# The end of a fused attention and convolution kernel reordered: quotients given out once their accumulators are complete, the last PV product ahead, output rows summed in banks of their own

## The chip, the cores and the metric

The kernel runs on one core of a Trainium2 chip. The metric is device time in microseconds, the median of three runs; lower is better. The program is one launch, about 51,000 instructions, written in a language in which each engine gets its instructions in the order in which the Python code issues them, and waits on semaphores for what other engines produce.

## The reference, cut to what matters

Two independent parts share the output: attention goes to columns 0 to 511, a long convolution to columns 512 to 1023.

```python
# A: 32 query heads of width 16 share one key and one value head; S = 2048, D = 512
q = (x @ wq).reshape(B, S, 32, 16).transpose(0, 2, 1, 3)
k, v = x @ wk, x @ wv
p = softmax(einsum("bhqd,bkd->bhqk", q, k) * 16 ** -0.5)
a = einsum("bhqk,bkd->bhqd", p, v).transpose(0, 2, 1, 3).reshape(B, S, 512) @ wo
# B: kv = (4-tap causal convolution of k) * v;  y = 2048-tap causal convolution of kv (by FFT) + kv * D
b = q_in * y
out = concatenate([a, b], axis=-1)
```

## The kernel before

**Stacks and tiles.** Attention is cut into 32 stacks: four chunks of 512 query rows, and in each chunk eight groups of four heads. A stack has 32 tiles (a few have 30). For one tile TensorE computes scores of 128 keys against two heads and 512 queries (`scores`, L934), ScalarE takes the exponential of the whole 128 x 1024 block (`exp`, L946), and TensorE multiplies by the values (`pv`, L970). The value matrix carries a column of ones, so the same product gives the softmax denominators. The last stack (number 31) is cut the other way: tiles 0 to 15 do all four heads for its first 256 queries, tiles 16 to 31 for its last 256. At the end of a stack, or of a half of the last one, VectorE adds the two accumulators into `ao` (L979, L980).

**Quotients.** For the stacks up to 29 numerators and denominators go through DRAM (`heads`). For the last two stacks `over` (L1190) does it on VectorE alone: six instructions on 128 x 256 (transpose, maximum, reciprocal, copy, transpose, product). Stack 30 (`ao2`) takes two calls, one for each half of its columns; stack 31 takes one for each half as it ends. The two halves of tile `lr` hold the quotients of stack 30 and of the first half of stack 31, tile `lb` those of its second half.

**Output rows.** The output projection (`wo`) adds up in `wp`, four tiles of 128 rows x 512 for the last chunk: heads of stacks 24 to 27 first, then of 28 and 29 (`wo_rows(i, [14])`, product `f<-wo,o`, VectorE L1171), then of stack 30 (product `f<-wl,lr`, VectorE L1184). `last` does the share of stack 31 after everything else: products of `lr` or `lb` with `wl` (L231), sums to `y`, four DMAs of 256 KB.

**Order.** `attend` (L1037) walks over the tiles. For tile x it issues the scores and the exponential of tile x+2, the planned `pv`, and then `fill.turn`, which lets a list of generator threads issue their own TensorE and VectorE work, as far as a slot's room goes. The first thread in the list that is willing goes first: `own` is first, `wo_part` sixth. A `yield` with a count asks for TensorE room, `yield 0, n` for VectorE time. Before, `own` ended after stack 30's special tile, and `wo_part` issued the calls of `over` for stack 30 and for the first half of stack 31 where they came in its own sequence.

**PSUM.** `wide` gives a two-bank tile of a pool with two buffers (tag `s`, shared with the scores), `pair` one of another pool with two buffers (tag `f`). In the last stack one `pair` is the accumulator of `pv` and the other goes from one filling product to the next, so a product that opens such a tile waits until VectorE has read the one before. The sums of `last` took three `wide` tiles in turn and one `pair`, each of which held one output row tile.

Of the kernel before, what the change touches and what calls it, by code (L numbers as in the profile page):

```python
# [8 lines left out]
F32 = mybir.dt.float32  # L9
# [5 lines left out]
ALU = mybir.AluOpType  # L15
# [4 lines left out]
P = 128  # L20
S = 2048
D = 512
H = 32
DH = 16
NKT = S // P
NQ = 4 * H // 4
CB = 256
# [78 lines left out]
WAIT = -1.0  # L106
# [3 lines left out]
class _Emit:  # L110
# [892 lines left out]
    def own(self):  # L1003

        nc, v = self.nc, self.nc.vector
        c = [x / TWO[5] * (-(2.0**18)) ** (5 - i) for i, x in enumerate(TWO)]
        self.vo = self.msk[:, 163:195]
        done = [f"q{c}" for c in range(4)]
        yield from self.after(*done)
        yield 0, 100  # L1010
        v.tensor_scalar(self.vo, self.vx[:, OWN, :], -TWO[5] * 2.0 ** (DOWN - 90), None, ALU.mult)
        room = [self.w.tile([P, 2, 4, 512], F16, tag="xt", bufs=2, name=self.nm("own")) for _ in range(2)]
        self.po = room[0].rearrange("p i k n -> p (i k n)").bitcast(F32).rearrange("p (a e n) -> p a e n", a=2, e=2)
        f = room[1].rearrange("p i k n -> p (i k n)").bitcast(F32).rearrange("p (a e n) -> p a e n", a=2, e=2)
        for n in OWN_IN:
            while self.slot < 32 * n - 32 + OWN_AT or self.owed:
                yield WAIT, 1
            for a in range(2):
                yield (1, 2400, CONT, 1, 4) if a else (1, 2400, NEW, 1)
                b = self.pair()  # L1020
                self.keys(b, n, OWN, a, slice(0, 512))
                v.tensor_scalar(self.po[:, a], b, MAGIC, None, ALU.add)
                v.scalar_tensor_tensor(f[:, a], self.po[:, a], MAGIC, b, ALU.subtract, ALU.subtract)
                if a == 0:
                    yield WAIT, 1.5, CONT
            for a in range(2):
                g, y = self.po[:, a], f[:, a]
                x = self.w.tile([P, 2, 512], I16, tag="s2", bufs=S2, name=self.nm("x"))
                yield 0, 900
                v.tensor_scalar(x, g, 2.0**-11, (127 - DOWN) * 128 - MAGIC * 2.0**-11, ALU.mult, ALU.add)  # L1030
                for i in range(4, -1, -1):
                    yield 0, 1220
                    v.scalar_tensor_tensor(g, g if i < 4 else y, c[i], y if i else x.bitcast(BF16), ALU.add, ALU.mult)  # L1033
            self.owed = [(-1 - n, part) for part in range(2)]
        self.seen.add("own")

    def attend(self, fill):  # L1037
        self.od = self.dr.tile([NQ, P, 512], F32, name="od")
# [82 lines left out]
    def wo_part(self):  # L1121
        nc, w, I = self.nc, self.w, self.I
        xr = self.out.rearrange("b (c p i) d -> (b c) p i d", c=4, p=P, i=4)
        for c in range(2):
            yield from self.after(("oc", 4 * c + 3), *[("cx", 1)] * c)
            for i in (0, 2):
                b = yield from self.wo_rows(i, range(4 * c, 4 * c + 4), 1400)
                for r in range(2):
                    t = self.s2("wp", (512,))
# [7 lines left out]
        for i in (0, 2):  # L1137
            b = yield from self.wo_rows(i, range(8, 11), 1400)
# [4 lines left out]
        for i in (0, 2):  # L1143
            b = yield from self.wo_rows(i, [11], 1400)
            for r in range(2):
                t = self.s2("wp", (512,))
# [7 lines left out]
        for i in (0, 2):  # L1154
            b = yield from self.wo_rows(i, range(12, 14), 1400)
# [4 lines left out]
        for q in range(2):  # L1160
            t = self.s2("wl", (512,))
            nc.gpsimd.memset(t, 0.0)
            for j in range(4):
                h = H - 8 + 4 * q + j
# [3 lines left out]
        for i in (0, 2):  # L1168
            b = yield from self.wo_rows(i, [14], 1400)
            for r in range(2):  # L1170
                nc.vector.scalar_tensor_tensor(self.wp[i + r], b[r], 1 / (OS * WS), self.wp[i + r], ALU.mult, ALU.add)  # L1171
        both = w.tile([P, 2, 4, 512], F32, tag="in", bufs=1, name="lr")
        t, self.lr = both[:, 0], both[:, 1]
        for h in range(2):
            while self.slot < 2 * NKT * (NQ - 1) + 1:
                yield WAIT, 1
            yield 0, 1800
            self.over(self.ao2[:, 256 * h : 256 * h + 256], t, h)
        halves = [slice(256 * h, 256 * h + 256) for h in range(2)]
        for i in (0, 2):  # L1180
            work = [[(h, t[:, 2, r * P : (r + 1) * P], self.wl[0][:, h]) for h in halves] for r in (i, i + 1)]
            b = yield from self.halves(*work, 2, 1400)
            for r in range(2):
                nc.vector.tensor_tensor(self.wp[i + r], self.wp[i + r], b[r], ALU.add)  # L1184
        while self.slot < 2 * NKT * (NQ - 1) + NKT:
            yield WAIT, 1
        yield 0, 1800
        self.over(self.ao[:, 0:256], self.lr, 0)

    def over(self, a, t, h):  # L1190

# [11 lines left out]
    def last(self, fill):  # L1203

        nc = self.nc
        xr = self.out.rearrange("b (c p i) d -> (b c) p i d", c=4, p=P, i=4)
        fill.finish()
        t = self.w.tile([P, 2, 4, 512], F32, tag="big", bufs=2, name="lb")[:, 0]
        self.pv(len(self.at) - 2, None)
        s = [self.wide()[:, 0, :]]  # L1210
        y = [self.s2("y", (512,)) for _ in range(4)]
        rows = lambda x, i: x[:, 2, i % 2 * P : (i % 2 + 1) * P]
        self.mm(s[0], rows(self.lr, 0), self.wl[1])
        self.pv(len(self.at) - 1, None, True)
        self.over(self.ao[:, 256:512], t, 0)
        s += [self.wide()[:, 0, :], self.wide()[:, 0, :], self.bank()]
        self.mm(s[1], rows(self.lr, 1), self.wl[1])
        self.mm(s[2], self.ident, self.wp[2], stop=False)
        for i in range(2, 4):
            self.mm(s[i], rows(t, i), self.wl[1], start=i > 2)  # L1220
        for i in range(2):
            nc.vector.tensor_tensor(y[i], self.wp[i], s[i], ALU.add)
        nc.scalar.copy(y[2], s[2])
        nc.vector.tensor_tensor(y[3], self.wp[3], s[3], ALU.add)
        for i in range(4):
            (nc.sync, nc.scalar)[i // 2 % 2].dma_start(xr[3][:, i, 0:D], y[i])


class _Fill:
# [226 lines left out]
```

## Time and profile before

| | us |
|---|---|
| median of three runs | 1016.74 (1013.69, 1016.74, 1018.21) |
| profiled execution, its own time | 1014.1 |
| its span, first to last instruction | 1012.3 |
| TensorE busy, share of the span | 947.4, 94% |
| ScalarE busy | 953.3, 94% |
| VectorE busy | 738.7, 73% |
| GpSimd busy | 172.0, 17% |
| mean granted TensorE clock | 0.989 |

In the rows of the timeline the columns are start, length (from the first start to the last end of the merged instructions), engine, line, operation, output and inputs, shape, count, and in brackets the idle time before it on that engine with what the profile takes for its releaser. "issue" is a wait that the profile ties to no other engine. One 512-column float32 product of L231 is four instructions in the order, one for each 32 output rows, and eight records in the trace. A table of windows gives busy time by engine in each stretch, then the granted TensorE clock as a share of full speed.

### The profile page before, as it was taken

How to read it: one execution, taken by the hardware profiler on the slowest of the kernel's cores; microseconds unless marked ns; L12 is line 12 of the kernel's file. 1: busy time of each engine (PE TensorE's matmuls, PEld its weight loads, DVE VectorE, ACT ScalarE, POOL GpSimd, SP SyncE). 2: the span in 40 equal slices, each digit the busy share in tenths (PEclk: the TensorE clock that was granted, in tenths of full speed). 3: DMA queues.
4: the chain of work that ended last, by engine and by line, in shares of the span. 5: the costliest groups of instructions: out<-in, count | busy, mean ns of one | idle time of the engine just before them, and what ended most of it. 6: DMA issues, size and time to landing. Idle time of an engine off the chain costs nothing.

```text
span 1012.3 us, 51279 instructions
## 1 busy us (share of the span) xinstructions
PE 947.4 (94%) x23439; PEld 463.1 (46%) x23439; DVE 738.7 (73%) x1009; ACT 953.3 (94%) x1034; POOL 172.0 (17%) x305
## 2 busy tenths in 40 slices
PE   8999999999999999999999989999889989998985
PEld 4344455444454444445554545544334445443452
DVE  4647866998538888989988858598999942866633
ACT  4699999999999999999999989999999999999982
POOL 2443111411003000101233434000000023200000
PEclk9899999999999999999999999999999999999998
DMA  7262333432123211122154424101211143310101
GB/s 231 92 190 75 119 103 102 107 99 84 46 75 78 70 53 54 53 90 75 55 152 123 126 86 124 54 22 47 70 37 43 42 126 115 92 56 25 42 4 46
DMA packets 69317, 83.12 MB, mean 82 GB/s; under 512 B 20800, under 2 KB 58278, under 8 KB 69094
## 3 DMA queue, kind: packets, MB, share of 16 engines
q1 hardware_dynamic: 47142, 43.51, 13.6%
q0 software_dynamic: 20320, 35.46, 11.8%
q8 instruction: 185, 3.03, 1.3%
q10 hardware_dynamic: 1632, 0.81, 0.3%
q14 instruction: 38, 0.31, 0.1%
HBM read 54.66 MB, written 25.03 MB: 79 GB/s over the span
## 4 chain that ended last, share of the span: by engine, by line
PE 56%; ACT 27%; DVE 9%; issue 7%; DMA 2%; POOL 0%; SPq 0%; ACTq 0%; DVEq 0%; POOLq 0%
ACT p L946 26%; PE f L970 26%; PE s L934 16%; PE f L249 12%; DVE own L1033 2%; DVE sp L169 1%; DMA xb<-in_A_x 1%; DVE ao L979 1%; PE x L231 0%; PE f L617 0%; DVE u L218 0%; DVE sp L289 0%; DVE sp L219 0%; DVE sp L220 0%; DVE ao L980 0%
## 5 line engine op out<-in xcount | busy, mean ns | idle before, releaser
L946 ACT ACTIVATE p<-s 128x1024 f32<-128x1024 f32 x1018 | 940.8, 1068 | 22.2 <-PE s L934 19.3
L970 PE MATMUL f<-p,vx 64*32 64x512 f32 (+1 forms) x8896 | 554.0, 556 | 1.7 <-DVE cut L683 1.1
L934 PE MATMUL s<-st,kst 49*32 49x512 f16 x8144 | 431.0, 382 | 31.2 <-ACT p L946 27.6
L934 PEld LDWEIGHTS <-kst 49*32 49x32 f16 x8192 | 199.0, 89 | 396.5 <-issue 355.4
L970 PEld LDWEIGHTS f<-p,vx 64*32 64x32 f32 x8896 | 178.3, 106 | 30.0 <-issue 4.3
L169 DVE TENSOR_TENSOR sp<-sp 128x1024 f32<-128x1024 f32 x96 | 111.3, 1214 | 0.0
L289 DVE COPY sp<-f 128x512 f32<-128x512 f32 x64 | 41.2, 685 | 63.8 <-PE f L249 63.8
L294 POOL DMA_DIRECT2D ff<-in_ff x64 | 34.5, 544 | 284.4 <-ACT p L946 282.1
L249 PE MATMUL f<-wo,o 64*32 64x512 f16 x1440 | 57.4, 375 | 3.8 <-DVE r L467 1.6
L979 DVE COPY ao<-f 128x512 f32<-128x512 f32 (+1 forms) x33 | 22.2, 673 | 50.3 <-PE f L970 50.3
L169 DVE TENSOR_TENSOR sp<-sp,sp 128x1024 f32<-128x1024 f32 x48 | 55.9, 1213 | 0.2
L249 PE MATMUL f<-xT,wq 64*32 64x512 f16 x1344 | 51.8, 375 | 1.6 <-DVE gm L729 1.3
L294 POOL DMA_DIRECT2D fi<-in_fi x32 | 17.6, 555 | 187.1 <-ACT p L946 187.1
L249 PE MATMUL f<-a,ff 64*32 64x256 f32 x1024 | 43.4, 382 | 4.6 <-DMA ff<-in_ff 3.4
L467 DVE TENSOR_TENSOR r<-f,q 128x256 f32<-128x256 f32 x32 | 12.1, 419 | 45.2 <-PE f L249 45.2
L249 PE MATMUL f<-hT,ff 64*32 64x256 f32 x1024 | 41.5, 377 | 1.2 <-PE s L934 0.3
L249 PE MATMUL f<-sp,fi 64*32 64x256 f32 x1024 | 40.4, 376 | 0.4 <-PE s L934 0.4
L469 POOL DMA_DIRECT2D out<-r x32 | 17.5, 552 | 106.2 <-DVE r L467 105.9
L404 DVE TENSOR_TENSOR a<-a,t 128x512 f32<-128x512 f32 x48 | 33.2, 691 | 1.6
L395 DVE TENSOR_TENSOR t<-kk,tpb 128x512 f32<-128x512 f32 (+1 forms) x50 | 32.9, 662 | 0.7 <-DMA qd<-qp 0.7
L249 PEld LDWEIGHTS <-o 64*32 64x32 f16 x1440 | 22.5, 93 | 19.0 <-DVE r L467 2.1
L322 POOL DMA_DIRECT2D hin<-in_B_ssm_k x32 | 21.1, 665 | 58.8 <-ACT p L946 57.4
(165 smaller groups left out, 726.5 us busy)
## 6 DMA issues: line engine op xcount, KB each, us to landing
ff<-in_ff POOLq DMA_DIRECT2D x64, 128.0 KB, 2.7
od<-ao SPq DMA_DIRECT2D x60, 128.0 KB
qd<-qp SPq DMA_DIRECT2D x48, 128.0 KB
st<-qd SPq DMA_DIRECT2D x62, 98.0 KB
kk<-in_B_k POOLq DMA_DIRECT2D x32, 128.0 KB, 3.0
v<-in_B_v POOLq DMA_DIRECT2D x32, 128.0 KB, 3.2
hin<-in_B_ssm_k POOLq DMA_DIRECT2D x32, 128.0 KB, 5.5
fi<-in_fi POOLq DMA_DIRECT2D x32, 128.0 KB, 3.4
```

Source lines behind the costliest of these rows:

```text
L169: v.tensor_tensor(part(out), part(a), part(b), op)
L249: y = self.nc.tensor.matmul(out[j : j + 32, cols], w[r, j : j + 32], x[r], start=half == m == 0, stop=half == 1 and m == k - 1,)
L289: self.nc.vector.tensor_copy(c[:, :, m + i, :], b[i].rearrange("p (q n) -> p q n", q=2))
L294: self.paced(self.nc.gpsimd.dma_start(t[:, i], self.I[n][:, 2 * m2 + i]))
L322: self.paced(nc.gpsimd.dma_start(dst, src))
L395: nc.vector.tensor_tensor(out[:, n], kk[:, x], tap(i, n.stop - n.start), ALU.mult)
L404: nc.vector.tensor_tensor(a, a, t, ALU.add)
L934: self.nc.tensor.matmul(s[j : j + 32, e, :], self.kst[rows, k * P + j : k * P + j + 32], self.st[n][rows, a, cols], start=True, stop=True,)
L946: self.exps[u % 4] = self.nc.scalar.activation(self.pt[u], s, AF.Exp, scale=LN2 * DH**-0.5 / SC / SC)
L970: nc.tensor.matmul(self.acc[e][32 * j : 32 * j + 32, m], vx[rows, :], y, start=k == 0, stop=stop)
L979: nc.vector.tensor_copy(a, self.acc[0][:, m])
L1033: v.scalar_tensor_tensor(g, g if i < 4 else y, c[i], y if i else x.bitcast(BF16), ALU.add, ALU.mult)
```

## The change

Three things move. The calls of `over` for stack 30 and for the first half of stack 31 are now issued by thread `own`, the first in the list, as soon as the walk has passed the tile that completes the accumulator; `wo_part` waits for the flag `"lt"` only. In `last`, the products for output rows 0 and 1 go to the two banks of one `pair`; the first of them stands ahead of the last two `pv`, and row 0 gets its `wp` by a product with the identity in place of a VectorE sum, as row 2 had already. The last `pv`, the sums into `ao` and `over` for `lb` follow, and on TensorE the products that don't need `lb` stand behind the last `pv` and ahead of those that do. Row 3 is done in two halves of 256 columns, each in a bank of its own `wide` tile with a DMA of its own; row 0 is copied out by ScalarE.

```diff
@@ own
         self.seen.add("own")
+        yield from self.after(("cx", 1))
+        both = self.w.tile([P, 2, 4, 512], F32, tag="in", bufs=1, name="lr")
+        self.lt, self.lr = both[:, 0], both[:, 1]
+        while self.slot < 2 * NKT * (NQ - 1) + 1:
+            yield WAIT, 0.5
+        for h in range(2):
+            yield 0, 1800
+            self.over(self.ao2[:, 256 * h : 256 * h + 256], self.lt, h)
+        self.seen.add("lt")
+        while self.slot < 2 * NKT * (NQ - 1) + NKT:
+            yield WAIT, 0.5
+        yield 0, 1800
+        self.over(self.ao[:, 0:256], self.lr, 0)
@@ wo_part
-        both = w.tile([P, 2, 4, 512], F32, tag="in", bufs=1, name="lr")
-        t, self.lr = both[:, 0], both[:, 1]
-        for h in range(2):
-            while self.slot < 2 * NKT * (NQ - 1) + 1:
-                yield WAIT, 1
-            yield 0, 1800
-            self.over(self.ao2[:, 256 * h : 256 * h + 256], t, h)
+        yield from self.after("lt")
...
-        while self.slot < 2 * NKT * (NQ - 1) + NKT:
-            yield WAIT, 1
-        yield 0, 1800
-        self.over(self.ao[:, 0:256], self.lr, 0)
@@ last
-        self.pv(len(self.at) - 2, None)
-        s = [self.wide()[:, 0, :]]
...
-        self.mm(s[0], rows(self.lr, 0), self.wl[1])
+        b = self.pair()
+        s = [b[:, 0, :], b[:, 1, :]]
+        self.mm(s[0], rows(self.lr, 0), self.wl[1], stop=False)
+        self.pv(len(self.at) - 2, None)
         self.pv(len(self.at) - 1, None, True)
         self.over(self.ao[:, 256:512], t, 0)
-        s += [self.wide()[:, 0, :], self.wide()[:, 0, :], self.bank()]
+        self.mm(s[0], self.ident, self.wp[0], start=False)
         self.mm(s[1], rows(self.lr, 1), self.wl[1])
+        s += [self.wide()[:, 0, :], self.wide()]
         self.mm(s[2], self.ident, self.wp[2], stop=False)
-        for i in range(2, 4):
-            self.mm(s[i], rows(t, i), self.wl[1], start=i > 2)
-        for i in range(2):
-            nc.vector.tensor_tensor(y[i], self.wp[i], s[i], ALU.add)
+        self.mm(s[2], rows(t, 2), self.wl[1], start=False)
+        nc.scalar.copy(y[0], s[0])
+        nc.sync.dma_start(xr[3][:, 0, 0:D], y[0])
+        nc.vector.tensor_tensor(y[1], self.wp[1], s[1], ALU.add)
+        nc.sync.dma_start(xr[3][:, 1, 0:D], y[1])
         nc.scalar.copy(y[2], s[2])
-        nc.vector.tensor_tensor(y[3], self.wp[3], s[3], ALU.add)
-        for i in range(4):
-            (nc.sync, nc.scalar)[i // 2 % 2].dma_start(xr[3][:, i, 0:D], y[i])
+        nc.scalar.dma_start(xr[3][:, 2, 0:D], y[2])
+        for i, h in enumerate((slice(0, CB), slice(CB, D))):
+            self.mm(s[3][:, i, 0:CB], rows(t, 3), self.wl[1][:, h])
+            nc.vector.tensor_tensor(y[3][:, h], self.wp[3][:, h], s[3][:, i, 0:CB], ALU.add)
+            nc.sync.dma_start(xr[3][:, 3, h], y[3][:, h])
```

Up to the last stack every engine has the same instructions in the same order with the same waits. Where they differ, the order of instructions shows it. VectorE before, from the sum of stack 30's accumulators (`ao`) to the first quotient of that stack (`lr`); `f_22028` and `f_22217` are the products of stacks 28 and 29 for output rows 0 and 1, and 2 and 3:

```order
L980 TENSOR_TENSOR ao_22064<-ao_22064,f_21475 128x512
L1171 SCALAR_TENSOR_TENSOR wp_20714<-f_22028,wp_20714 128x512
L1171 SCALAR_TENSOR_TENSOR wp_20715<-f_22028,wp_20715 128x512
L1171 SCALAR_TENSOR_TENSOR wp_20716<-f_22217,wp_20716 128x512
L1171 SCALAR_TENSOR_TENSOR wp_20717<-f_22217,wp_20717 128x512
L1195 STREAM_TRANSPOSE lr<-ao_22064 128x256
L1197 TENSOR_SCALAR lr<-lr 128x8
L1198 RECIPROCAL lr<-lr 128x8
L1199 COPY lr<-lr 128x256
L1200 STREAM_TRANSPOSE lr<-lr 128x256
L1201 TENSOR_TENSOR lr<-ao_22064,lr 128x256
```

The same place on VectorE now (`f_22029` is what was `f_22028`):

```order
L980 TENSOR_TENSOR ao_22065<-ao_22065,f_21475 128x512
L1198 STREAM_TRANSPOSE lr<-ao_22065 128x256
L1200 TENSOR_SCALAR lr<-lr 128x8
L1201 RECIPROCAL lr<-lr 128x8
L1202 COPY lr<-lr 128x256
L1203 STREAM_TRANSPOSE lr<-lr 128x256
L1204 TENSOR_TENSOR lr<-ao_22065,lr 128x256
L1184 SCALAR_TENSOR_TENSOR wp_20714<-f_22029,wp_20714 128x512
L1184 SCALAR_TENSOR_TENSOR wp_20715<-f_22029,wp_20715 128x512
```

The first quotient stands ahead of the sums for rows 0 and 1; the second, of the other 256 columns, stands behind them and ahead of the sums for rows 2 and 3. In the same way the quotient of stack 31's first half now stands ahead of the four sums that add stack 30 to `wp`, where it stood behind them.

TensorE at the end before, from the third-last `pv` on; `p_22810` is the last exponential's output, `x` tiles come from `wide`, `f` tiles from `pair`:

```order
L970 MATMUL f_22544<-p_22756,vx 32x256 x8
L970 MATMUL f_22544<-p_22775,vx 32x256 x8
L231 MATMUL x_22829<-wl_21929,lr 32x512 x4
L970 MATMUL f_22544<-p_22810,vx 32x256 x8
L231 MATMUL x_22854<-wl_21929,lr 32x512 x4
L231 MATMUL x_22855<-wp_20716,ident 32x512 x4
L231 MATMUL x_22855<-wl_21929,lb 32x512 x4
L231 MATMUL f_22856<-wl_21929,lb 32x512 x4
```

And now (`f_22825` is the new pair for rows 0 and 1, which takes the buffer of the last filling product; `x_22863` is row 3's tile):

```order
L970 MATMUL f_22550<-p_22762,vx 32x256 x8
L231 MATMUL f_22825<-wl_21930,lr 32x512 x4
L970 MATMUL f_22550<-p_22781,vx 32x256 x8
L970 MATMUL f_22550<-p_22810,vx 32x256 x8
L231 MATMUL f_22825<-wp_20714,ident 32x512 x4
L231 MATMUL f_22825<-wl_21930,lr 32x512 x4
L231 MATMUL x_22862<-wp_20716,ident 32x512 x4
L231 MATMUL x_22862<-wl_21930,lb 32x512 x4
L231 MATMUL x_22863<-wl_21930,lb 32x256 x8
```

One 512-column product with the identity is added. The row-0 product stands ahead of two `pv` in place of one, and three products that don't need `lb` stand together behind the last `pv`. Of the eight instructions of the last row the first four are row 3's first half and the others its second; by its semaphores the second half waits for the VectorE sum that reads the first half out of the same tile. The first row's product waits for the last VectorE sum that reads the filling product before it.

More of the change, by code (lines that the diff above doesn't have):

```diff
@@ L1171, in wo_part @@
                 nc.vector.scalar_tensor_tensor(self.wp[i + r], b[r], 1 / (OS * WS), self.wp[i + r], ALU.mult, ALU.add)
-        both = w.tile([P, 2, 4, 512], F32, tag="in", bufs=1, name="lr")
-        t, self.lr = both[:, 0], both[:, 1]
-        for h in range(2):
-            while self.slot < 2 * NKT * (NQ - 1) + 1:
-                yield WAIT, 1
-            yield 0, 1800
-            self.over(self.ao2[:, 256 * h : 256 * h + 256], t, h)
+        yield from self.after("lt")
         halves = [slice(256 * h, 256 * h + 256) for h in range(2)]
         for i in (0, 2):
-            work = [[(h, t[:, 2, r * P : (r + 1) * P], self.wl[0][:, h]) for h in halves] for r in (i, i + 1)]
+            work = [[(h, self.lt[:, 2, r * P : (r + 1) * P], self.wl[0][:, h]) for h in halves] for r in (i, i + 1)]
             b = yield from self.halves(*work, 2, 1400)
```

## The prediction

> **What bounds the kernel now.** The page first: ScalarE's exponentials, one per tile, fill the span.
>
> ```profile
> span 1012.3 us, 51279 instructions
> L946 ACT ACTIVATE p<-s 128x1024 f32<-128x1024 f32 x1018 | 940.8, 1068 | 22.2 <-PE s L934 19.3
> ```
>
> They take 940.8 of 1012.3 us, with 22.2 us of idle time ahead of them. Up to the last stack no instruction changes its place, so only that stack and what follows the last exponential can move. There I read ScalarE's timeline from 970 us on:
>
> ```profile
> 970.81 1.97 ACT L946 ACTIVATE p<-s 128x1024 f32<-128x1024 f32 x2
> 975.22 1.94 ACT L946 ACTIVATE p<-s 128x1024 f32<-128x1024 f32 x2 [2.44 <-PE s L934]
> 978.22 15.09 ACT L946 ACTIVATE p<-s 128x1024 f32<-128x1024 f32 x16 [1.05 <-PE s L934]
> 1005.42 0.59 ACT L1223 COPY y<-x 128x512 f32<-128x512 f32 x1 [12.11 <-PE x L231]
> ```
>
> Three facts: a hole of 2.44 us, a second of 1.05, and a last exponential that ends at 978.22 + 15.09 = 993.31. From there to the end, 1012.3 - 993.31 = 19.0 us, no exponential is left. The holes wait for scores, so TensorE's timeline comes next, and with it VectorE's.
>
> ```profile
> 965.66 0.41 PE L934 MATMUL s<-st,kst 49*32 49x512 f16 x8
> 966.32 0.41 PE L249 MATMUL f<-wo,o 64*32 64x512 f16 x8
> 966.53 0.41 PE L934 MATMUL s<-st,kst 49*32 49x512 f16 x8
> 971.22 0.63 PE L970 MATMUL f<-p,vx 64*32 64x256 f32 x16
> 974.05 0.64 PE L249 MATMUL f<-wl,lr 64*32 64x256 f32 x10 [2.21 <-issue]
> 991.91 1.20 PE L970 MATMUL f<-p,vx 64*32 64x256 f32 x32
> 995.57 1.65 PE L231 MATMUL x<-wl,lr 128*32 128x512 f32 x8 [2.46 <-issue]
> 997.15 1.11 PE L970 MATMUL f<-p,vx 64*32 64x256 f32 x16
> 998.19 1.60 PE L231 MATMUL x<-wl,lr 128*32 128x512 f32 x8
> 1002.18 1.45 PE L231 MATMUL x<-wp,ident 128*32 128x512 f32 x8 [2.39 <-DVE y L1222]
> 1003.33 2.01 PE L231 MATMUL x<-wl,lb 128*32 128x512 f32 x8
> 1005.03 1.63 PE L231 MATMUL f<-wl,lb 128*32 128x512 f32 x8
> ```
>
> ```profile
> 962.18 0.69 DVE L980 TENSOR_TENSOR ao<-ao,f 128x512 f32<-128x512 f32 x1
> 970.48 1.29 DVE L1171 SCALAR_TENSOR_TENSOR wp<-f,wp 128x512 f32<-128x512 f32 x2 [6.38 <-PE f L249]
> 971.69 0.43 DVE L1195 STREAM_TRANSPOSE lr<-ao 128x256 f32<-128x256 f32 x1
> 973.42 0.42 DVE L1201 TENSOR_TENSOR lr<-ao,lr 128x256 f32<-128x256 f32 x1
> 975.49 0.43 DVE L1201 TENSOR_TENSOR lr<-ao,lr 128x256 f32<-128x256 f32 x1
> 980.14 0.42 DVE L980 TENSOR_TENSOR ao<-ao,f 128x256 f32<-128x256 f32 x1
> 992.00 1.28 DVE L1184 TENSOR_TENSOR wp<-wp,f 128x512 f32<-128x512 f32 x2 [9.96 <-PE f L249]
> 994.94 0.42 DVE L1201 TENSOR_TENSOR lr<-ao,lr 128x256 f32<-128x256 f32 x1
> 998.37 0.42 DVE L979 COPY ao<-f 128x256 f32<-128x256 f32 x1 [3.00 <-PE f L970]
> 1001.02 0.42 DVE L1201 TENSOR_TENSOR lb<-ao,lb 128x256 f32<-128x256 f32 x1
> 1001.36 1.28 DVE L1222 TENSOR_TENSOR y<-wp,x 128x512 f32<-128x512 f32 x2
> 1006.72 0.69 DVE L1224 TENSOR_TENSOR y<-wp,f 128x512 f32<-128x512 f32 x1 [4.08 <-PE f L231]
> ```
>
> Two waits of TensorE are called "issue", but both end 0.21 us behind a quotient: `lr` is done at 973.42 + 0.42 = 973.84 and the product that reads it starts at 974.05; the third quotient is done at 994.94 + 0.42 = 995.36 and its product starts at 995.57. So I take both for waits on a quotient that VectorE made late. Stack 30's accumulators were summed by 962.18 + 0.69 = 962.87, and VectorE then stood idle for 6.38 us behind a sum for `wp` before it began. The third wait, 2.39 us before 1002.18, is for a PSUM buffer that the sum of L1222 reads.
>
> The third thing is the clock, in windows:
>
> ```profile
> 910.58:913.99 3.41, 2.10 (x64) 0.82 (x43) 3.38 (x5) 3.30 (x4) 0.00 (x0) 1.00 0.02 5
> 972.02:975.43 3.41, 1.38 (x52) 1.07 (x60) 3.10 (x11) 0.97 (x2) 0.00 (x0) 1.00 0.00 0
> 975.43:978.84 3.41, 3.41 (x80) 2.10 (x72) 0.45 (x2) 2.35 (x3) 0.00 (x0) 0.50 0.02 5
> 992.49:995.91 3.42, 0.96 (x28) 0.33 (x24) 2.70 (x8) 0.82 (x1) 0.00 (x0) 1.00 0.02 5
> 995.91:999.32 3.41, 3.41 (x32) 0.43 (x24) 0.89 (x3) 0.00 (x0) 0.00 (x0) 0.50 0.00 0
> 999.32:1002.73 3.41, 1.02 (x12) 0.30 (x12) 3.15 (x8) 0.00 (x0) 0.00 (x0) 1.00 0.00 0
> 1002.73:1006.15 3.42, 3.42 (x24) 0.85 (x15) 0.00 (x0) 0.59 (x1) 0.00 (x0) 0.50 0.45 161
> ```
>
> The granted clock (the figure behind POOL's) falls to half for exactly one window of 3.41 us after each window in which TensorE was busy for only 1.38, 0.96 or 1.02 us. After a window with 2.10 us busy, 910.58 on, it did not fall. So the bound of "too idle" lies between 1.3 and 2.0 us of idleness in 3.41. The second hole of ScalarE, 1.05 us, lies in such a half-clock window, and the products of L231 run 1.70 us at half clock (1003.33 to 1005.03), so 0.85 at full.
>
> [...]
>
> **The change, part by part.** All in the time of the profiled execution.
>
> *First quotients (stack 30).* VectorE now starts the first one at 962.9. Its length, 971.69 to 973.84, is 2.15 us, and the second, done at 975.49 + 0.43 = 975.92, took 2.08 more while TensorE and ScalarE ran again. So: first quotient done at 965.05, sums for rows 0 and 1 (1.29) at 966.3, second quotient at 968.4, 2.1 us before TensorE brings the sums for rows 2 and 3 at 970.48. Behind those sums there is now no quotient. The product at 974.05 then waits only for its buffer, which the sums free at 970.48 + 1.29 = 971.77; with 0.2 it starts at 971.97, where TensorE comes free at 971.22 + 0.63 = 971.85, and 0.12 is left. Both holes go: 2.44 + 1.05 = 3.49. New waits: the product at 966.32 needs the buffer that the sums for rows 0 and 1 free at 966.3, so it slips to 966.5, 0.17 us, with scores and exponentials queued behind it; and the 0.12 above. If ScalarE's queue of scores hides nothing of these, 3.49 - 0.29 = **3.2 us**. From below I take 2.9 (each wait twice as long), from above 3.9: the 16 exponentials in 15.09 us are 0.943 each, against 0.917 for the ten tiles between 981.45 and 990.61, where TensorE's scores keep step, and 16 x 0.026 = 0.4 of that may be recovered too.
>
> ```profile
> 981.45 0.41 PE L934 MATMUL s<-st,kst 49*32 49x512 f16 x8 [0.52 <-ACT p L946]
> 985.76 0.63 PE L249 MATMUL f<-wl,lr 64*32 64x256 f32 x16
> 990.61 0.41 PE L934 MATMUL s<-st,kst 49*32 49x512 f16 x8
> ```
>
> *Quotient of stack 31's first half.* It now follows the sum that ends at 980.14 + 0.42 = 980.56, and the two sums that add stack 30 to rows 0 and 1 come behind it: 980.56 + 2.15 + 1.29 = 984.0. The product that needs their buffer started at 985.76, so 1.7 us are left and the cost is nothing; a quotient longer by more than that would make TensorE wait.
>
> *The tail*, counted from the last exponential at 993.31 and with the old times, as everything shifts alike. The product for row 0 stands behind the third-last `pv` (991.91 + 0.63 = 992.5) and waits for its buffer, which the sums at 992.00 free at 993.28; with 0.21 it starts at 993.49, after a wait of 1.0 us. Three terms at full clock: product 0.96 (its 1.58 us from 995.57 to 997.15 were 0.34 at full and 1.24 at half clock), `pv` 0.52 (997.15 to 998.19, halved), `pv` 0.52 and 0.1 of drain (998.19 to 998.37, halved): the first sum into `ao` starts at 995.6, where it started at 998.37. Then, as before, 3.07 us to `lb` (998.37 to 1001.02 + 0.42 = 1001.44): 998.7 in place of 1001.44. Meanwhile TensorE does three products of 0.85, 995.5 to 998.05: hidden under the 3.07, with 0.85 to spare, and that cover is gone at half clock. Behind `lb`: 0.2 wait, row 2's product 0.85, row 3's first half 0.43 + 0.28 of drain (1005.03 to 1006.72 is 1.13 at full clock, less 0.85), its sum 0.42 (as the 256-column sum at 980.14), 0.2, second half 0.71, sum 0.42: 1002.2. Before, the last sum ended at 1006.72 + 0.69 = 1007.41. Row 1's sum (0.69) lies on VectorE ahead of row 3's and ends at 999.4, before that is wanted; row 0's and row 2's copies are on ScalarE, 0.59 each, where nothing else is queued. So 1007.41 - 1002.2 = **5.2 us**. What lies behind the last sum, 1012.3 - 1007.41 = 4.9 us, I keep: SP's queue holds four of the five DMAs, but the three ahead of the last are issued at least 0.9 us earlier, and two of 256 KB kept the DMA engines busy for 0.45 of 3.42 us (the window at 1002.73), 0.8 us each. The last one moves half as much, which could save up to 0.4. Tail: 5.2, from 3.3 (a half-clock window over the two `pv`, below) to 5.6.
>
> Sum 3.2 + 5.2 = **8.4 us**. Against the profiled execution: 1014.1 - 8.4 = 1005.7. That execution and the three runs (1013.69 to 1018.21) have a mean of 1015.7, which I take as the level: 1015.7 - 8.4 = **1007.3 us**; against the median alone it would be 1008.3.
>
> **The rivals.**
>
> *A: half clock in the tail after all.* The 1.0 us wait before row 0's product, with what else a window holds, reaches the bound (1.3 to 2.0). One half-clock window over the product and the two `pv` costs 0.96 + 1.04 = 1.9 us, one over the work behind `lb` as much again, 0.85 + 0.43 + 0.43 = 1.7. Gain 6.5 or 4.8: 1009.2 to 1010.9. For it: 0.96 to 1.38 us busy did trip it thrice. Against it: 2.4 us of work are left in that window, and 2.10 did not trip it. [...]
>
> *B: "issue" is meant literally.* Then the waits of 2.21 and 2.46 us are TensorE's own and stay; only the third wait, 2.39, and part of what follows goes, 8.4 - 3.2 - 2.5 = 2.7 us: 1013.0. For it is the name in the row, against it the two distances of 0.21 us behind a quotient.
>
> *C: VectorE late.* If the quotient takes 1.3 us longer while ScalarE and TensorE run at full rate, the product at 966.32 waits 1.5 us, enough for the clock, and the first term shrinks to 3.49 - 1.47 - 0.12 - 1.05 = 0.9 us: 1009.6. Against it: the second quotient, 2.08 us beside running engines.
>
> *D: half clock that doesn't lift.* If the short new waits kept each window at the bound, a tile of 0.87 us on TensorE (965.66 to 966.53) takes 1.74 against ScalarE's 0.917, and a window of 3.41 us yields 1.96 tiles in place of 3.72: 1.6 us lost. From six windows on that eats the 8.4 us; all seven from 966 to 990 cost 11.2, the tail's products and `pv` (0.96 + 1.04 + 0.85 + 0.86) another 3.7, so 1015.7 + 14.9 - 8.4 = 1022.2. Against it: one busy window lifted it each time here.
>
> **How the numbers follow.** Forecast 0.73, A 0.15, B 0.05, C 0.05, D 0.02. A measurement of this kernel can tell about 0.5% (5.1 us) from no change, so the border is 1011.7. Faster takes the forecast, A and C, less some for a level that can lie 2 us off: 0.88. Same takes B and that rest: 0.10. Slower is D: 0.02. The low end is the lowest run less the upper terms, 1013.7 - 3.9 - 5.6 = 1004.2; the high end is the median less A's smaller gain, 1016.74 - 4.8 = 1011.9; outside lie B, D and the rest of a bad level.
>
> **What would show it.** In the changed trace: no hole over 0.5 us between the exponentials from 960 us on, and clock 1.00 there; the first product with `lr` within 0.3 us of the `pv` before it; a wait of about 1 us before row 0's product; from the last exponential to the end 13.8 us in place of 19.0. Wrong would be a hole near the first `wo` product of rows 2 and 3, a half-clock window after the last exponential, or waits called "issue" of over 2 us at the same two places.

## The result, and the profile after

The changed kernel takes 1008.9 us (median of 17 runs, 1006.21 to 1013.64) against 1016.74 (17 runs beside it, 1012.68 to 1019.36): a ratio of 0.9931, 95% interval 0.9918 to 0.9944. The forecast was 1007.3 in a range of 1004.2 to 1011.9, faster. The profiled execution of the changed kernel took 1007.08 us.

The page's span and its line of exponentials, after:

```profile
span 1005.3 us, 51318 instructions
L946 ACT ACTIVATE p<-s 128x1024 f32<-128x1024 f32 x1018 | 940.4, 1068 | 20.4 <-PE s L934 17.5
```

ScalarE's exponentials in the timeline of the changed kernel, from 952 us on:

```profile
952.71 21.35 ACT L946 ACTIVATE p<-s 128x1024 f32<-128x1024 f32 x23 [0.82 <-PE s L934]
974.38 16.61 ACT L946 ACTIVATE p<-s 128x1024 f32<-128x1024 f32 x18 [0.33 <-PE s L934]
```

The holes of 2.44 and 1.05 us are gone; one of 0.33 is left there. The last exponential ends at 974.38 + 16.61 = 990.99, and 14.3 us remain to the end, where it was 19.0. TensorE and VectorE at the same places:

```profile
967.59 0.41 PE L249 MATMUL f<-wo,o 64*32 64x512 f16 x8
972.49 0.63 PE L970 MATMUL f<-p,vx 64*32 64x256 f32 x16
973.25 0.80 PE L249 MATMUL f<-wl,lr 64*32 64x256 f32 x15
983.44 0.63 PE L249 MATMUL f<-wl,lr 64*32 64x256 f32 x16
991.17 1.07 PE L231 MATMUL f<-wl,lr 128*32 128x512 f32 x8 [0.96 <-issue]
992.17 1.09 PE L970 MATMUL f<-p,vx 64*32 64x256 f32 x32
996.50 1.50 PE L231 MATMUL x<-wl,lb 128*32 128x512 f32 x16 [0.52 <-DVE lb L1204]
998.54 0.64 PE L231 MATMUL x<-wl,lb 128*32 128x256 f32 x8 [0.55 <-DVE y L1233]
```

```profile
963.40 0.69 DVE L980 TENSOR_TENSOR ao<-ao,f 128x512 f32<-128x512 f32 x1
964.12 0.45 DVE L1198 STREAM_TRANSPOSE lr<-ao 128x256 f32<-128x256 f32 x1
965.87 0.42 DVE L1204 TENSOR_TENSOR lr<-ao,lr 128x256 f32<-128x256 f32 x1
966.21 1.28 DVE L1184 SCALAR_TENSOR_TENSOR wp<-f,wp 128x512 f32<-128x512 f32 x2
980.33 1.28 DVE L1191 TENSOR_TENSOR wp<-wp,f 128x512 f32<-128x512 f32 x2
989.68 1.29 DVE L1191 TENSOR_TENSOR wp<-wp,f 128x512 f32<-128x512 f32 x2 [8.08 <-PE f L249]
996.02 0.42 DVE L1204 TENSOR_TENSOR lb<-ao,lb 128x256 f32<-128x256 f32 x1
998.07 0.42 DVE L1233 TENSOR_TENSOR y<-wp,x 128x256 f32<-128x256 f32 x1 [1.02 <-PE x L231]
999.25 0.42 DVE L1233 TENSOR_TENSOR y<-wp,x 128x256 f32<-128x256 f32 x1 [0.76 <-PE x L231]
```

The first quotient is complete at 965.87 + 0.42 = 966.29, seven microseconds before the product that reads it. That product starts 0.13 us behind the end of the `pv` ahead of it (973.12). Row 0's product in the tail still waits, 0.96 us, but for its buffer, which the sums free at 989.68 + 1.29 = 990.97, 0.20 us ahead of it. The last sum ends at 999.67. The windows around both places give the granted clock, the figure behind the five engines' busy times:

```profile
971.00:980.00 9.00, 8.36 (x288) 5.39 (x273) 3.72 (x10) 8.67 (x11) 0.00 (x0) 1.00 0.03 5
990.00:1000.00 10.00, 7.15 (x96) 1.93 (x88) 5.25 (x13) 2.16 (x4) 0.00 (x0) 1.00 0.23 86
```

It is 1.00 in both, so TensorE did not fall to half speed there.

To compare stages rather than spans, the end of the program is cut at three points that every trace has: the start of the sum that completes stack 30's accumulators (963.40 above, 962.18 before), the end of the last exponential, and the end of the last sum into `y`. Each line is one profiled execution, and as the span is given to 0.1 us, the last two columns are good to 0.05.

| us | stack 30's sum | to the last exponential | on to the last sum | on to the span's end | last exponential to end |
|---|---|---|---|---|---|
| before | 962.18 | 31.13 | 14.10 | 4.89 | 18.99 |
| after | 963.40 | 27.59 | 8.68 | 5.63 | 14.31 |
| quotients alone | 965.71 | 27.58 | 10.49 | 5.62 | 16.11 |
| end alone | 964.20 | 31.15 | 12.81 | 5.74 | 18.55 |
| before, TensorE kept busy | 963.47 | 29.66 | 14.13 | 5.04 | 19.17 |
| after, sums delayed | 965.90 | 28.82 | 8.68 | 5.50 | 14.18 |
| after, sums delayed more | 962.30 | 31.18 | 8.69 | 5.63 | 14.3 |
| after, row 3 whole | 964.55 | 27.87 | 8.19 | 5.79 | 13.98 |
| after, row 3 apart | 965.82 | 27.57 | 7.92 | 6.19 | 14.11 |
| after, `pv` first | 965.62 | 27.62 | 7.25 | 5.81 | 13.06 |
| both of these | 964.54 | 28.05 | 6.50 | 6.31 | 12.81 |
| both, two queues | 963.72 | 27.75 | 6.51 | 5.82 | 12.33 |
| both, one DMA | 967.36 | 28.08 | 6.49 | 5.87 | 12.36 |

The first column differs by up to 5.2 us although no instruction ahead of it is moved: one execution's span says little about a few microseconds, the stages behind it say more. The change gains 31.13 - 27.59 = 3.54 us up to the last exponential and 14.10 - 8.68 = 5.42 up to the last sum, and loses 5.63 - 4.89 = 0.74 behind that: 8.2 us in all.

### The profile page after: what moved, and what is told of

Its sections match the earlier page's. It is cut to its first block, busy times and chain, and to the rows that moved or that the text cites. A ratio compares the mean times of both kernels' runs of the same rounds, so it can differ in the third digit from the quotient of the medians.

```text
span 1005.3 us, 51318 instructions
## 1 busy us (share of the span) xinstructions
PE 945.1 (94%) x23455; PEld 463.3 (46%) x23455; DVE 738.5 (73%) x1009; ACT 953.6 (95%) x1035; POOL 172.1 (17%) x305
## 3 DMA queue, kind: packets, MB, share of 16 engines
q1 hardware_dynamic: 47430, 43.78, 13.8%
q8 instruction: 185, 3.03, 1.3%
## 4 chain that ended last, share of the span: by engine, by line
PE 54%; ACT 28%; DVE 9%; issue 6%; DMA 2%; POOL 0%; SPq 0%; ACTq 0%; DVEq 0%; POOLq 0%
ACT p L946 27%; PE f L970 25%; PE s L934 15%; PE f L249 12%; DVE own L1033 2%; DVE sp L169 1%; DMA xb<-in_A_x 1%; DVE ao L979 1%; DVE sp L289 1%; DMA qd<-qp 1%; PE f L617 0%; DVE u L218 0%; DVE ao L980 0%; DVE sp L219 0%; DVE sp L220 0%
```

## The experiments

### Which of the two edits carries what

The changed kernel with the old `last`, so that only the quotients are early:

```diff
@@ last
+        self.pv(len(self.at) - 2, None)
+        s = [self.wide()[:, 0, :]]
...
-        b = self.pair()
-        s = [b[:, 0, :], b[:, 1, :]]
-        self.mm(s[0], rows(self.lr, 0), self.wl[1], stop=False)
-        self.pv(len(self.at) - 2, None)
```

> The quotients are given out early as in the changed kernel, the end (last) is that of the kernel before. Theory (TensorE waited on late quotients; three of its waits hang on them, two in the last stack and one after it): both holes between exponentials go (3.5 us), and the wait of 2.46 us ahead of row 0's product goes too, since that quotient is then also early; only the wait for the PSUM buffer of row 2 is left. The first sum of the last accumulators comes about 1.3 us behind the last exponential in place of 5.1, the last sum about 10.3 in place of 14.1. Some 7 us below the kernel before. Rival (the new order of the end carries the 4.7 us behind the last exponential): 3.5 us below, last sum still 14 us behind the last exponential.

And the other way round, the kernel before with the new `last` (the same lines, plus for minus):

> The end (last) is that of the changed kernel, the quotients come late as in the kernel before. Theory: both holes stay (2.4 and 1.1 us), row 0's product still waits for its late quotient, and now two products with the values stand behind it in place of one; last sum about 12.7 us behind the last exponential in place of 14.1; some 1 us below the kernel before. Rival (the new order of the end carries the gain there): last sum 8.7 us behind the last exponential, some 5 us below.

The quotients alone took 1009.86 us (4 runs; ratio 0.9932, 0.9906 to 0.9957), the end alone 1016.61 (10 runs; 0.9991, 0.9973 to 1.0009). Rows of ScalarE, TensorE and VectorE, and the windows, with the quotients alone:

```profile
976.68 16.61 ACT L946 ACTIVATE p<-s 128x1024 f32<-128x1024 f32 x18 [0.38 <-PE s L934]
993.03 1.06 PE L231 MATMUL x<-wl,lr 128*32 128x512 f32 x8
998.61 1.06 PE L231 MATMUL x<-wp,ident 128*32 128x512 f32 x8 [2.93 <-DVE y L1225]
1003.09 0.69 DVE L1227 TENSOR_TENSOR y<-wp,f 128x512 f32<-128x512 f32 x1 [4.03 <-PE f L231]
996.19:999.60 3.41, 0.99 (x12) 0.47 (x16) 2.73 (x7) 0.00 (x0) 0.00 (x0) 1.00 0.07 25
999.60:1003.01 3.41, 3.41 (x20) 0.57 (x11) 0.00 (x0) 0.58 (x1) 0.00 (x0) 0.50 0.40 145
```

And with the end alone:

```profile
977.86 1.02 ACT L946 ACTIVATE p<-s 128x1024 f32<-128x1024 f32 x1 [3.00 <-PE s L934]
997.61 1.93 PE L231 MATMUL f<-wl,lr 128*32 128x512 f32 x8 [3.03 <-issue]
999.48 1.96 PE L970 MATMUL f<-p,vx 64*32 64x256 f32 x32
```

With the quotients alone the large hole ahead of the last 18 exponentials is gone (0.38), and so is the wait of 2.46 us before row 0's product (993.03): 3.6 of the tail's 5.4 us (14.10 to 10.49) come with the quotients. What the old end keeps is the wait of 2.93 us for a buffer and, behind the window with 0.99 us of work, half clock. The new end removes these, 10.49 to 8.68, or 1.8 us. With the end alone the holes stay (3.00, 0.26 and 0.41 us, where 2.4 and 1.1 were expected), and row 0's product still waits for its late quotient, now 3.03 us since it stands one `pv` earlier. That product and the two `pv` behind it run at half clock (1.93 and 1.96 us, against 1.07 and 1.09 in the changed kernel): 1.3 us up to the last sum are left (14.10 to 12.81), and nothing that the times can tell. The rival in both expectations, that the end carries most of the tail, is refuted.

The shares depend on the order in which the two edits are counted. With the end first, it brings 1.3 us and the quotients 12.81 - 8.68 = 4.1. By the times alone the quotients make up the whole change (a ratio of 0.9932 against 0.9931): the 1.8 us of the new end stand on the stages of single traces.

### Is the second hole the clock's?

The kernel before with nine products of 128 x 512 put ahead of the first product that reads a quotient, into the same bank, which that product then overwrites. They remove no wait; they only give TensorE something to do in it.

```diff
@@ halves
+                    if fill is not None:
+                        self.warm(banks[0], fill, 9)
@@ wo_part
-            b = yield from self.halves(*work, 2, 1400)
+            b = yield from self.halves(*work, 2, 1400, None if i else self.oc[14][:, 0])
```

> The kernel before, with nine products of 128x512 in half precision put on TensorE (their output is overwritten) right ahead of the first product that reads a quotient, where TensorE stood idle for 2.2 us. Theory (the granted clock falls because TensorE was idle, and the second hole of 1.05 us comes from the clock alone): the first hole stays at 2.4 to 2.7 us, the clock stays at 1.00 in the 5 us behind it, the second hole goes; some 1 us below the kernel before. Rival (the second hole is the backlog of the first, whatever the clock): two holes, no difference.

Rows of ScalarE and TensorE, and a window; the line numbers are two higher here:

```profile
976.52 16.61 ACT L948 ACTIVATE p<-s 128x1024 f32<-128x1024 f32 x18 [2.28 <-PE s L936]
973.32 2.12 PE L569 MATMUL f<-o 128*128 128x512 f16 x9
975.44 0.76 PE L251 MATMUL f<-wl,lr 64*32 64x256 f32 x16
973.00:983.00 10.00, 9.48 (x265) 5.88 (x250) 6.20 (x17) 7.72 (x10) 0.00 (x0) 1.00 0.01 3
```

The first hole stays at 2.28 us, the second is gone, the clock is 1.00 throughout, and the stage is 31.13 - 29.66 = 1.5 us shorter: 1013.75 us (10 runs), ratio 0.997, interval 0.9953 to 0.9987. The rival is refuted. So of the 3.5 us some 1.5 were the price of half clock after the wait, and keeping TensorE at work on nothing useful gets that part alone.

### How late may VectorE be?

The price of rival C: in the changed kernel VectorE does two idle sums of 128 x 512 (or three) between the sum for row 2 and the sum for row 3 that frees the next buffer, so that TensorE's first product with `lr` waits for its buffer.

```diff
@@ wo_part
+                if i and r == 0:
+                    for _ in range(2):
+                        nc.vector.tensor_tensor(self.lr[:, 3], self.wp[0], self.wp[1], ALU.add)
```

> The changed kernel with two more VectorE sums of 128x512 (0.69 us each, into a place that nothing reads) between the two sums for rows 2 and 3, so that the buffer of the first product with a quotient comes free 1.4 us later. Theory (TensorE then waits about 1.5 us; idle time between 1.3 and 2.0 us in a window is where the clock may fall, and the nearer row, 1.31 us, did not): hole between exponentials 1.7 us, clock 1.00, 1.4 us above the changed kernel. Rival (VectorE late is enough to trip the clock): half clock for one window behind it, a second hole of about 1 us, 2.4 us above.

> As sums_delayed, with three VectorE sums in place of two, so that TensorE waits 2.2 us ahead of the first product with a quotient, as long as in the kernel before. Theory (idle time alone trips the clock, between 1.5 and 2.0 us in a window): half clock for one window of 3.41 us behind the wait, unless the window's edge splits the wait, and a second hole between exponentials of about 1 us: 3.4 us from the first hole and 1 to 2 from the second, against 1.6 in sums_delayed. Rival (half clock needs something else of the kernel before): one hole of 2.3 us, clock 1.00.

With two (1010.62 us, 5 runs; ratio 0.9948, 0.9923 to 0.9974), rows of ScalarE and TensorE and two windows:

```profile
978.11 2.86 ACT L946 ACTIVATE p<-s 128x1024 f32<-128x1024 f32 x3 [1.61 <-PE s L934]
977.03 0.76 PE L249 MATMUL f<-wl,lr 64*32 64x256 f32 x16 [1.48 <-issue]
974.34:977.76 3.42, 1.95 (x71) 1.20 (x60) 2.44 (x4) 2.15 (x3) 0.00 (x0) 1.00 0.00 0
977.76:981.17 3.41, 3.41 (x131) 2.62 (x122) 0.11 (x1) 3.06 (x4) 0.00 (x0) 1.00 0.02 5
```

With three (one run, 1009.55 us beside one of 1015.56 for the kernel before, which is too few to compare times):

```profile
976.16 1.02 ACT L946 ACTIVATE p<-s 128x1024 f32<-128x1024 f32 x1 [3.02 <-PE s L934]
974.43 1.21 PE L249 MATMUL f<-wl,lr 64*32 64x256 f32 x16 [2.22 <-issue]
970.75:974.16 3.41, 1.46 (x54) 0.68 (x37) 3.21 (x5) 2.39 (x3) 0.00 (x0) 1.00 0.00 0
974.16:977.57 3.41, 3.14 (x64) 2.72 (x72) 0.06 (x1) 1.15 (x2) 0.00 (x0) 0.50 0.02 5
```

A wait of 1.48 us costs what it lasts, less a little: 28.82 - 27.59 = 1.23 us, at full clock, near the 1.4 expected; the rival is refuted for a wait of this length. A wait of 2.22 us, only 0.74 longer, costs another 31.18 - 28.82 = 2.36 us in its one trace: a window with 1.46 us of work is followed by one at half clock. The 2.36 - 0.74 = 1.6 us above the longer wait agree with the 1.5 us that keeping TensorE busy won. The first hole was 3.02 us and two small ones of 0.26 and 0.24 followed, where 3.4 and about 1 were expected. This gives back the whole 3.5 us of the first term (31.18 against 31.13 before) although only one wait was made longer.

With three sums the window ahead of the half clock (970.75 to 974.16) held 1.95 us of idleness, 3.41 - 1.46. With two, the window at the same place (974.34 to 977.76) held 1.47, 3.42 - 1.95, and the clock stayed at 1.00. These two figures do not make a bound, as other windows of the trace with two sums show:

```profile
366.77:370.18 3.41, 1.80 (x64) 0.84 (x62) 3.38 (x6) 3.41 (x4) 0.00 (x0) 1.00 0.25 79
370.18:373.60 3.42, 3.42 (x56) 1.76 (x64) 3.35 (x7) 1.19 (x2) 0.00 (x0) 0.50 0.28 74
916.32:919.74 3.42, 1.79 (x56) 0.75 (x56) 3.39 (x5) 2.02 (x3) 1.80 (x4) 1.00 0.16 56
919.74:923.15 3.41, 3.41 (x96) 1.62 (x88) 3.08 (x3) 3.36 (x5) 0.28 (x1) 1.00 0.08 25
```

A window with 1.80 us of TensorE work was followed by half clock, one with 1.79 was not. So the busy time of a window does not decide by itself, and what else counts is not shown.

### What the new end still leaves

Four versions of the changed `last`. Row 3 in one piece, as before:

```diff
-        for i, h in enumerate((slice(0, CB), slice(CB, D))):
-            self.mm(s[3][:, i, 0:CB], rows(t, 3), self.wl[1][:, h])
...
+        self.mm(s[3], rows(t, 3), self.wl[1])
+        nc.vector.tensor_tensor(y[3], self.wp[3], s[3], ALU.add)
+        nc.sync.dma_start(xr[3][:, 3, 0:D], y[3])
```

> The changed kernel with row 3 in one piece: one product of 512 columns, one sum, one DMA of 256 KB. Theory (the second half's product waits for the sum that reads the first half out of the same tile, so the split lengthens the chain): from the start of row 2's last product to the end of the last sum 2.7 us in place of 3.2, the last DMA moves twice as much (0.4 us); time the same within 0.5 us. Rival (the split shortens the end as it looks): 0.5 us or more above the changed kernel, last sum later.

Row 3's halves in banks of two different tiles:

```diff
-        s += [self.wide()[:, 0, :], self.wide()]
+        s += [self.wide()[:, 0, :], self.wide()[:, 0, :], self.bank()]
...
-            self.mm(s[3][:, i, 0:CB], rows(t, 3), self.wl[1][:, h])
+            self.mm(s[3 + i][:, 0:CB], rows(t, 3), self.wl[1][:, h])
```

> The changed kernel with the two halves of row 3 in two tiles (one of the wide pool, one of the pair pool). Theory: the second half's product no longer waits for the sum of the first (0.55 us of idle TensorE ahead of it goes), from the start of row 2's last product to the end of the last sum 2.4 us in place of 3.2; 0.8 us below the changed kernel. Rival (the pair's buffer is freed too late, or the wait is of another origin): 3.2 us as before.

Row 0's product behind the last `pv`, so that its wait no longer holds up the sums into `ao`:

```diff
-        self.mm(s[0], rows(self.lr, 0), self.wl[1], stop=False)
         self.pv(len(self.at) - 2, None)
         self.pv(len(self.at) - 1, None, True)
         self.over(self.ao[:, 256:512], t, 0)
+        self.mm(s[0], rows(self.lr, 0), self.wl[1], stop=False)
```

> The changed kernel with row 0's first product behind both of the last two products with the values, in place of ahead of them. Theory (that product waits for the buffer of the last filling product, 0.96 us in the trace, and both products with the values queue behind it, though the last exponential is done by then): the first sum of the last accumulators starts 0.8 us behind the last exponential in place of 2.4; the four products without lb end at the same time as lb, so the last sum comes 7.2 us behind the last exponential in place of 8.7; 1.5 us below the changed kernel. Rival (the four products then end behind lb and take the gain back): 8.2 us or more.

And the last two together:

> Both: row 0's product behind the last products with the values, and row 3's halves in tiles of their own. Theory: the two add up, last sum 6.4 us behind the last exponential in place of 8.7; 2.3 us below the changed kernel, about 10 us (1.0%) below the kernel before. Rival (the end is set by something else, the DMAs or what follows them): no more than 1 us below the changed kernel.

TensorE's last row with row 3 apart, the product of the second half, which has no wait ahead of it:

```profile
1000.21 0.61 PE L231 MATMUL f<-wl,lb 128*32 128x256 f32 x8
```

TensorE with both, the last `pv`:

```profile
992.64 0.67 PE L970 MATMUL f<-p,vx 64*32 64x256 f32 x16 [0.25 <-ACT p L946]
```

Up to the last sum all four came out as expected: 8.19, 7.92, 7.25 and 6.50 us against 8.68. The split of row 3 thus lengthens that chain by 0.5 us, because its second half waits 0.55 us for a sum that reads the other bank of the same tile. That wait is one that the program's semaphores ask for; with tiles apart it is gone. The `pv` first is worth 1.4 us: with it the last `pv` waits for its exponential alone (0.25), where the changed kernel's wait of 0.96 stood ahead of it. From the last exponential to the end, though, the four show only 13.98, 14.11, 13.06 and 12.81 against 14.31. Row 3 apart gains 0.76 and gives back 0.56 behind the last sum, and both together gain 1.5 us where 2.3 were expected and the rival allowed 1. By the times: 1008.51 (2 runs; ratio 0.9925, 0.99 to 0.9951), 1008.35 (2; 0.9924, 0.9897 to 0.995), 1007.44 (4; 0.991, 0.9888 to 0.9931) and 1007.28 us (6; 0.9911, 0.9894 to 0.9928).

### Where that is given back

With row 3 apart its two sums end 0.43 us after one another, and so do the DMAs behind them. The view of L1234 (smallest, median and largest time of the issuing instruction in ns) of the changed kernel, and of the one with both:

```profile
L1234 SPq DMA_DIRECT2D out<-y x2: 332/332/332, 998.5 to 999.7; - x2
```

```profile
L1234 SPq DMA_DIRECT2D out<-y x2: 332/850/1369, 998.7 to 999.1; - x2
```

The second issue takes 1.37 us in place of 0.33. ScalarE's queue had issued row 2's DMA just ahead of the two:

```profile
998.42 0.37 ACTq L1230 DMA_DIRECT2D out<-y  x1
```

So the slow one is the third within 0.7 us (998.42, 998.7, 999.1). Two versions of "both" take that apart, one with the second half's DMA on ScalarE's queue, one with a single DMA for the row:

```diff
-            nc.sync.dma_start(xr[3][:, 3, h], y[3][:, h])
+            (nc.sync, nc.scalar)[i].dma_start(xr[3][:, 3, h], y[3][:, h])
```

> PV first and row 3 apart, and the second half's DMA of row 3 issued by ScalarE's queue, not SP's. In the version with both on SP the second issue took 1.37 us right behind the first, where an issue by itself takes 0.33, and 6.31 us passed from the last sum to the end. If the queue is what took the time: that issue takes about 0.37 us, and last sum to end is 5.3 us, last exponential to end 11.8 in place of 12.81. Rival, the time behind the last sum is that of the transfers and of the program's end: it stays at 6.3, and the last exponential to the end at 12.8.

```diff
-            nc.sync.dma_start(xr[3][:, 3, h], y[3][:, h])
+        nc.sync.dma_start(xr[3][:, 3, 0:D], y[3])
```

> PV first and row 3 apart, with one DMA of 256 KB for row 3 behind both sums. If the second issue's wait behind the first took the time: the one issue takes 0.33 us, last sum to end is 5.3 to 5.6 us, last exponential to end 11.8 to 12.1 in place of 12.81. Rival, that the last 256 KB move later and so land later: last sum to end stays at 6.3 or grows, and two DMAs were right.

The same line with two queues, and with one DMA:

```profile
L1234 ACTq DMA_DIRECT2D out<-y x1: 1540/1540/1540, 998.0 to 998.0; - x1
```

```profile
L1234 SPq DMA_DIRECT2D out<-y x1: 332/332/332, 1002.0 to 1002.0; - x1
```

The expectation missed for the first: the issue is as slow on the other queue (1.54 us), again as the third within 0.7 us, so one queue's order is not the reason; and yet the end comes 0.49 us sooner (6.31 to 5.82). With one DMA the issue is short, and the end comes no sooner than that (5.87, where 5.3 to 5.6 was expected). Each gets back 0.44 to 0.49 us of the 0.68 by which the end of "both" is longer than that of the changed kernel. Times: 1006.55 (4 runs; ratio 0.9922, 0.9902 to 0.9941) and 1007.08 us (4; 0.9921, 0.99 to 0.9942). The version with two queues has the shortest end by the trace, 12.33 us in place of 14.31; the intervals of the six versions and of the changed kernel overlap.

What ends the program shows in SP's own instructions. Behind its last DMA SP goes through a branch (the kernel's `if` that skips a general version) and then through eight waits on semaphores, by their times those of the output DMAs among them. These are its branch and its waits, with the time of the first and the last, before:

```profile
L1433 SPq COMPARE_BRANCH  x1: 53/53/53, 1003.1 to 1003.1; - x1
L1433 SPq EVENT_SEMAPHORE  x8: 17/17/17, 1006.1 to 1010.6; - x8
```

And in the changed kernel:

```profile
L1441 SPq COMPARE_BRANCH  x1: 53/53/53, 1000.1 to 1000.1; - x1
L1441 SPq EVENT_SEMAPHORE  x8: 17/17/17, 1003.1 to 1003.6; - x8
```

From SP's branch to its next instruction it takes 3.0 us in both (1003.1 to 1006.1, and 1000.1 to 1003.1). Before, ScalarE's queue issues the last two DMAs, so SP branches early, and then waits until 1010.6 for their landing (their packets move until 1009.9). In the changed kernel SP itself issues the last DMA, at 999.7, and branches behind it; once it gets to its eight waits it is through in 0.5 us, so no DMA holds it up for more than a moment. Behind the last sum there stand then the issue, the 3.0 us from branch to next instruction, and 2.2 us from the first wait to the end of the span. With both edits, the slow issue of 1.37 us stands on SP ahead of its branch (1000.5), which comes 1.4 us behind the last sum in place of 0.4; the next instruction follows 2.6 us behind the branch (1003.1, the last wait at 1003.7), so some 0.6 us of the delay remain. With two queues it stands on ScalarE, SP branches at 998.0, and its waits run from 1001.2 to 1002.1. So in these traces the long issue cost more on SP, which still had its branch and its waits ahead of it (6.31 us from the last sum to the end), than on ScalarE (5.82).

## Why the prediction was right

**What bounds the kernel.** The two waits called "issue" were waits for a quotient. Given early, both go (quotients alone: 0.38 us of hole, no wait before row 0's product); left late, both stay (end alone: a hole of 3.00 us and a wait of 3.03). Rival B is refuted.

**First quotients.** 3.2 us forecast, 3.54 measured. The quotient's length (2.17 us, from 964.12 to 966.29; 2.15 forecast) and the end of the sums for rows 0 and 1 (967.49, 4.09 us behind the start of stack 30's sum; 966.3 - 962.18 = 4.12 forecast) held. The slip at the first `wo` product of rows 2 and 3 was 0.05 us, not 0.17 (967.59 - 963.40 = 4.19 behind stack 30's sum, 4.14 before). The new hole is 0.33 us for the 0.29 of the two waits. The term came out low by something that the prediction had put into its upper end only: the exponentials behind the holes came at 15.09 / 16 = 0.943 us before and at 16.61 / 18 = 0.923 now, 16 x 0.020 = 0.32 us. 3.49 - 0.33 + 0.32 = 3.48 of the 3.54.

**Quotient of stack 31's first half** at nothing: the two sums behind it end at 980.33 + 1.28 = 981.61, and the product that needs their buffer starts at 983.44 with no wait. 1.8 us were left, 1.7 were forecast.

**The tail.** 5.2 us forecast, 5.42 measured up to the last sum, with the expected wait of 1.0 us before row 0's product (0.96) and the clock at 1.00 (rival A did not come). The 0.2 us more lie behind `lb`, which was done 5.45 us behind the last exponential (996.44 - 990.99; 998.7 - 993.31 = 5.4 forecast): two waits that the sum had at 0.2 us each measured 0.06 (996.50 - 996.44) and 0.05 (998.54 - 998.49). What the prediction did not say is whose gain it is: 3.6 us of it come with the quotients alone, and the rewritten end adds 1.8.

Mis-sized is the step that keeps 4.9 us behind the last sum: it measured 5.63, 0.74 more, so that from the last exponential to the end there are 14.3 us where 13.8 were forecast. The 4.9 us were those of a program whose last DMA ScalarE issues while SP already waits; with the new end SP issues it and reaches its waits 3.0 us behind its branch, as shown above. That the quotients alone, with the four old DMAs, have 5.62 us too is another matter: there SP waits for the landing of ScalarE's DMA as before (its waits end at 1007.7, 3.9 us behind the issue at 1003.81; before at 1010.6, 3.2 us behind 1007.44). Why that landing came 0.7 us later is not tested.

**Rival C's price.** A wait of 1.5 us at the product of rows 2 and 3 was taken as enough for the clock. A wait of 1.48 us, at the first product with `lr`, was not; one of 2.22 was. In that place the point from which the rival decides was put too low, by up to 0.7 us.

**The prediction's rule for the clock.** That a window of little TensorE work is followed by half clock, for one window, held at every place in the last stack where the prediction used it. As a rule it is too simple. Windows with 1.80 and 1.79 us of work went different ways, as shown above, and in the trace before, at the program's start, the window from 29.93 us had 3.30 us of work and was followed by two at half clock, of which the first (33.35 to 36.76) was busy throughout. With the end alone a half-clock window with 2.49 us of work (996.69 to 1000.10) was followed by another. So what stood against rival D, that one busy window lifts the clock, is not safe either; D itself did not come, as the clock of 1.00 from 971 to 980 us shows.

**The level.** 1015.7 less 8.4 gave 1007.3; the median of 17 runs before is 1016.74, and less the stages' 8.2 that is 1008.5, against 1008.9 measured. The lower level, taken from four executions, is the larger part of the 1.6 us by which the forecast was low. That 8.4 lies so near the 8.2 us of the stages is partly luck: the first two terms were 0.3 and 0.2 us too small, and the end behind the last sum 0.7 us longer than assumed.

## What to carry to other kernels

Where a wait is called "issue", look for the instruction of another engine that ended just before it, and for where that engine stood idle earlier: here work for the end of the program could have been done 6 us sooner, in a gap, and giving it out on completion of its input was worth most of the change. A wait of 2.22 us on TensorE cost 3.6 us here, through the clock, and one of 1.48 us cost 1.2: the first 0.74 us taken off it were worth more than all the rest. Ask of the last DMA not only when it is issued but by which engine, and what that engine has to do before the program ends: here SP's next instruction came 3.0 us behind its branch. Undo each half of a change alone: gains that both halves seem to bring in one stage may hang on one of them.

## What the hardware showed beside that

- In one place 1.47 us of idleness in a window of 3.42 us left the clock at 1.00 (two sums more) and 1.95 us in one of 3.41 was followed by a window at half speed (three sums more), and 0.74 us more of waiting cost 2.36 us. Elsewhere in the trace with two sums a window with 1.80 us of work was followed by half speed and one with 1.79 was not.
- SP's next instruction came 3.0 us behind its branch before and in the changed kernel, and 2.6 us behind it with both of the later edits.
- The third of three output DMAs issued within 0.7 us took 1.37 us to issue on SP's queue (both edits) and 1.54 on ScalarE's (two queues), where the two ahead of it took 0.33 to 0.37.
- The same instructions reached stack 30's sum between 962.18 and 967.36 us in thirteen traces.
